# Rewriting a four-layer attention kernel: features on partitions, blocks of tokens through both layer kinds, softmax without a max pass

## The chip, the cores and the metric

One core of a Trainium2 chip. The metric is the device time of one execution in microseconds (us), slowest core; with one core that is the core. Each kernel ran several times beside runs of the kernel before on the same chip. Engines: PE is TensorE (PEld its weight loads), DVE is VectorE, ACT is ScalarE, POOL is GpSimd, SP is SyncE.

## The reference, cut to what matters

`x` is 2048 tokens by 512 features, bf16, 32 heads of 16. Four layers A, B, A, B, each with a layer norm before it and a residual after it.

```python
def _A_ref(x, wqkv, w_phi, wo):                 # linear attention
    q, k, v = ...                               # x @ wqkv, split into 32 heads of 16
    pq, pk = q @ w_phi, k @ w_phi               # per head
    phi_q = concat([softmax(pq), softmax(-pq)]) # 32 features per head
    phi_k = concat([softmax(pk), softmax(-pk)])
    kv, z = phi_k.T @ v, phi_k.sum(tokens)      # over ALL tokens
    o = (phi_q @ kv) / (phi_q @ z + 1e-6)
    return o @ wo
def _B_ref(x, wqkv, wo):                        # window of 8 tokens, every second one back
    logits[s, w] = q[s] . k[s - 2 * w] * 16 ** -0.5   # masked where s - 2w < 0
    o[s] = sum_w softmax(logits[s])[w] * v[s - 2 * w]
    return o @ wo
x = x + _A_ref(_layernorm(x), ...)   # then B, A, B
```

Layer A holds a barrier: no numerator before the key-value sum of all tokens is complete.

## The kernel before

Tokens sit on partitions: 128 tokens, 512 features along the free dimension, four such tiles to a "quad". One layer runs after the other.

```python
def s1():                                   # layer A: max and min of each head's 16, then subtract
    nc.vector.tensor_tensor(out=mm[:, 0], in0=v[:, :, 0:8, :], in1=v[:, :, 8:16, :], op=ALU.max)
    nc.vector.tensor_tensor(out=mm[:, 1], in0=v[:, :, 0:8, :], in1=v[:, :, 8:16, :], op=ALU.min)
    # ... three more tree steps for each sign, then two subtractions into dd (cut)
def s_a():                                  # layer B: logits of one tile
    nc.vector.tensor_tensor(out=prod, in0=st["Q"][:, i:i + 1, :].to_broadcast([P, NW, D]),
                            in1=Kall[:, _win(j), :], op=ALU.mult)          # 4096 wide
    for d in range(nd_):                    # sum over a head's 16 by identity matmuls, 256 columns
        nc.tensor.matmul(lg[:, i, :, :], lhsT=ident[:], rhs=prod[:, :, d * H:(d + 1) * H], ...)
def s_c():                                  # layer B: values
    nc.vector.tensor_tensor(out=pav, in0=..., in1=attn[...], op=ALU.mult)  # 4096 wide
    for cb in range(NB):
        for w in range(NW):                 # 32 identity matmuls of 128 columns
            nc.tensor.matmul(oTp[:, cb, :], lhsT=pavf[:, w, cb * P:(cb + 1) * P], rhs=ident[:], ...)
def residual_out(oT, Wo, j):
    # 4 matmuls with Wo, a fifth with the identity adds x, ScalarE copies the sum back (cut)
```

A shifted token lies on another partition, so keys and values also pass through shifted-row copies by DMA.

## Time and profile before

| | before |
|---|---|
| median of the first runs (three, and one more beside the changed kernel) | 567.5 us (565.6 to 569.8) |
| PE / DVE / ACT busy | 429.7 / 410.8 / 315.4 us |
| granted TensorE clock, profiled run | 0.91 |

### The profile page before, as it was taken

To read this page: it belongs to the slowest core of one execution; us is meant where nothing else is said; L and a number is where in the kernel's file an instruction comes from. 1 tells how busy PE (TensorE), PEld (TensorE's weight loads), DVE (VectorE), ACT (ScalarE), POOL (GpSimd) and SP (SyncE) were. 2 spreads that over 40 slices of the span, in tenths; PEclk is the share of its full clock that TensorE was granted. 3 is DMA by queue.
4 is the path that set the end of the run, shared out by engine and by line. 5 is a ranking of instruction groups with operands and counts; after the bars stand their busy time and mean duration, and the time that the engine had idled before them with its cause. 6 is when DMAs were issued, how large, how long until landed. Compare 5 with 4: busy or idle time off the path is not lost.

```text
span 567.9 us, 7855 instructions
## 1 busy us (share of the span) xinstructions
PE 429.7 (76%) x3153; PEld 265.6 (47%) x3196; DVE 410.8 (72%) x582; ACT 315.4 (56%) x529; POOL 2.7 (0%) x16
## 2 busy tenths in 40 slices
PE   0337778607897999999898687633797999999983
PEld 0213334307443666656763243223553566666762
DVE  1975799986563489886994599997672669584970
ACT  0086787832497346283458867843488535454241
POOL 1000000000000000000000000000000000000000
PEclk9999797855898999999999888966898999999998
DMA  9851030344255302022013003313544322002003
GB/s 239 203 118 34 1 74 1 74 74 111 55 135 128 75 2 65 2 62 42 1 39 70 5 2 74 74 45 74 107 105 112 80 56 59 8 14 53 1 1 149
DMA packets 98020, 37.22 MB, mean 66 GB/s; under 512 B 88512, under 2 KB 97216, under 8 KB 97728
## 3 DMA queue, kind: packets, MB, share of 16 engines
q1 hardware_dynamic: 96320, 35.66, 27.2%
q10 hardware_dynamic: 1664, 1.07, 0.8%
q8 instruction: 25, 0.41, 0.3%
q14 instruction: 11, 0.09, 0.0%
HBM read 5.26 MB, written 2.10 MB: 13 GB/s over the span
## 4 chain that ended last, share of the span: by engine, by line
DVE 39%; PE 30%; ACT 19%; issue 7%; DMA 3%; SPq 1%; ACTq 0%; DVEq 0%
PE ps_arena L298 11%; PE ps_arena L364 6%; DVE arena L355 6%; DVE arena L524 5%; PE ps_arena L306 5%; ACT arena L282 5%; DVE arena L406 5%; PE ps_arena L415 4%; ACT arena L505 3%; DVE arena L498 3%; DVE arena L496 3%; PE ps_arena L572 2%; ACT arena L300 2%; DVE stat L250 2%; ACT x_sb L310 2%
## 5 line engine op out<-in xcount | busy, mean ns | idle before, releaser
L298 PEld LDWEIGHTS <-arena 128*128 128x128 bf16 x768 | 78.6, 103 | 159.4 <-issue 74.6
L300 ACT CAST arena<-ps_arena 128x512 bf16<-128x512 f32 x192 | 110.5, 584 | 61.8 <-PE ps_arena L298 56.5
L298 PE MATMUL ps_arena<-WA,arena 128*128 128x512 bf16 x375 | 101.1, 426 | 50.1 <-ACT arena L300 37.2
L355 DVE TENSOR_TENSOR arena<-arena 128x4096 bf16<-128x4096 bf16 x32 | 71.8, 2286 | 35.3 <-ACT arena L300 33.0
L298 PE MATMUL ps_arena<-WB,arena 128*128 128x512 bf16 x372 | 90.0, 388 | 8.5 <-ACT arena L300 7.8
L406 DVE TENSOR_TENSOR arena<-arena 128x4096 bf16<-128x4096 bf16 x32 | 71.5, 2285 | 0.4
L505 ACT ACTIVATE arena<-arena 128x4096 bf16<-128x4096 bf16 x16 | 57.9, 3618 | 15.4 <-DVE arena L498 15.1
L415 PE MATMUL ps_arena<-ident,arena 128*128 128x128 bf16 x1024 | 63.1, 219 | 1.8 <-DVE arena L406 1.7
L415 PEld LDWEIGHTS <-arena 128*128 128x128 bf16 x1024 | 59.5, 98 | 10.4 <-DVE arena L406 3.8
L364 PE MATMUL ps_arena<-arena,ident 128*128 128x256 bf16 x512 | 60.5, 272 | 1.7 <-DVE arena L355 0.7
L250 DVE BATCH_NORM_STATS2 stat<-x_sb 128x6 f32<-128x512 bf16 x64 | 43.4, 684 | 24.8 <-ACT x_sb L310 24.6
L364 PEld LDWEIGHTS <-ident 128*128 128x128 bf16 x512 | 50.0, 98 | 13.7 <-issue 5.4
L310 ACT CAST x_sb<-ps_arena 128x512 bf16<-128x512 f32 x64 | 37.1, 580 | 34.5 <-PE ps_arena L309 34.5
L282 ACT ACTIVATE arena<-x_sb,nmr,rstd 128x512 bf16<-128x512 bf16 x64 | 49.3, 809 | 5.3 <-DVE nmr L274 4.8
L536 PE MATMUL ps_arena<-arena 128*128 128x136 bf16 x256 | 22.6, 265 | 30.7 <-DVE arena L524 30.6
L524 DVE TENSOR_TENSOR arena<-arena 128x4096 bf16<-128x4096 bf16 x16 | 36.6, 2286 | 5.4 <-ACT arena L522 5.4
L306 PEld LDWEIGHTS <-arena 128*128 128x128 bf16 x256 | 22.5, 99 | 33.8 <-ACT arena L419 11.6
L536 PEld LDWEIGHTS <-arena 128*128 128x128 bf16 x256 | 21.4, 121 | 34.2 <-DVE arena L524 33.1
L306 PE MATMUL ps_arena<-WoB,arena 128*128 128x512 bf16 x113 | 29.9, 381 | 8.2 <-ACT arena L419 6.0
L306 PE MATMUL ps_arena<-WoA,arena 128*128 128x512 bf16 x124 | 33.8, 387 | 0.5 <-issue 0.2
L572 PE MATMUL ps_arena<-arena 128*128 128x136 bf16 x256 | 25.5, 263 | 11.3 <-DVE arena L582 7.8
L377 ACT CAST arena<-ps_arena 128x1024 bf16<-128x1024 f32 x8 | 8.1, 1012 | 42.0 <-PE ps_arena L367 42.0
(61 smaller groups left out, 355.6 us busy)
## 6 DMA issues: line engine op xcount, KB each, us to landing
arena<-arena SPq DMA_DIRECT2D x8, 448.0 KB
arena<-arena SPq DMA_DIRECT2D x8, 336.0 KB
x_sb<-in_A_x_dram SPq DMA_DIRECT2D x1, 2048.0 KB
out_dram<-x_sb SPq DMA_DIRECT2D x1, 2048.0 KB
arena<-in_B_wqkv_dram SPq DMA_DIRECT2D x1, 1536.0 KB
arena<-arena SPq DMA_DIRECT2D x8, 105.0 KB
arena<-in_A_wqkv_dram ACTq DMA_DIRECT2D x1, 512.0 KB
arena<-arena SPq DMA_TRANSPOSE x32
```

Of the source, the lines that this page charges most:

```text
L250: nc.vector.bn_stats(out=stat[:, i, :], in_=x_sb[:, j, :])
L282: nc.scalar.activation(out=xn[:, i, :], in_=x_sb[:, j, :], func=ACT.Identity, scale=st["rstd"][:, i:i + 1], bias=st["nmr"][:, i:i + 1])
L298: nc.tensor.matmul(ps, lhsT=XNT[:, POS[j], c, :], rhs=W[:, c, col0:col0 + D], start=(c == 0), stop=(c == NB - 1))
L300: nc.scalar.copy(out=dst, in_=ps)
L306: nc.tensor.matmul(y, lhsT=oT[:, c, :], rhs=Wo[:, c, :], start=(c == 0), stop=(c == NB - 1 and not pe_res))
L310: nc.scalar.copy(out=x_sb[:, j, :], in_=y)
L355: nc.vector.tensor_tensor(out=prod, in0=st["Q"][:, i:i + 1, :].to_broadcast([P, NW, D]), in1=Kall[:, _win(j), :], op=ALU.mult)
L364: nc.tensor.matmul(lg[:, i, :, :], lhsT=ident[:], rhs=prod[:, :, d * H:(d + 1) * H], start=(d == 0), stop=(d == nd_ - 1 and not masked))
L406: nc.vector.tensor_tensor(out=pav, in0=Vall[:, _win(j), :].rearrange("p w (d h) -> p w d h", h=H), in1=attn[:, j, :, :].unsqueeze(2).to_br ...
L415: nc.tensor.matmul(oTp[:, cb, :], lhsT=pavf[:, w, cb * P:(cb + 1) * P], rhs=ident[:], start=(w == 0), stop=(w == NW - 1))
L505: nc.scalar.activation(out=ee, in_=st["dd"], func=ACT.Exp)
L524: nc.vector.tensor_tensor(out=phi, in0=ee, in1=rsb.to_broadcast([P, 2, G, DH, 8]), op=ALU.mult)
```

## The change

The intent: put features on partitions, so that a shifted token is a shifted column and needs no copy; let indicator matmuls sum over the features of a head; drop the max pass of both softmaxes (a check at the end sends unfit data to the old kernel, kept as a general path); cut the tokens into four blocks of 512 and lead each block from A into B and on into the next A, with the order of each engine's instructions set by hand through virtual times. The core of the diff, cut:

```diff
+class _Fast:
+    def g_a1(self, L, b):                       # keys and values of block b, layer A
+        for t in range(4):                      # ... projection into pk (cut)
+            nc.scalar.activation(out=E[:, t, 0, :], in_=pk[:], func=ACT.Exp)
+            nc.scalar.activation(out=E[:, t, 1, :], in_=pk[:], func=ACT.Exp, scale=-1.0)
+        # ... head sums on VectorE, scaling of E, then key-value sums over the block (cut)
+    def g_a2(self, L, b):                       # queries
+        # ... projection, two exponentials per chunk from PSUM (cut)
+        yield 0.5
+        S = self.ps()                           # head sums by 32-column indicator matmuls
+    def g_a3(self, L, b):                       # denominators, then scaling of the queries
+    def g_out(self, key, b, Wo, last, dt):
+        for t in range(4):                      # ... 4 matmuls with Wo into y (cut)
+            nc.vector.scalar_tensor_tensor(out=xb[:, t, :], in0=y[:], scalar=1.0, in1=xb[:, t, :],
+                                           op0=ALU.mult, op1=ALU.add, accum_out=sums[:, t:t + 1])
+            if t < 3:
+                yield dt
+        yield 0.8
+        for t in range(4):                      # layer norm: squares with their sum on ScalarE
+            nc.scalar.activation(out=sqd[:], in_=xb[:, t, :], func=ACT.Square, bias=nmean[:, t:t + 1],
+                                 accum_out=ss[:, t:t + 1])
+    def g_b2(self, L, b, dt):                   # logits and softmax of layer B
+        for c in range(NB + 1):                 # ... product with the shifted view of K (cut)
+            nc.tensor.matmul(lg[hf][32 * g:32 * g + 32, :], lhsT=self.indQK[:],
+                             rhs=prods[c - 1][:, hf * 4 + g, :], ..., tile_position=(0, 32 * g))
+        nc.scalar.activation(out=E[:, hf, :], in_=lg[hf][:], func=ACT.Exp, scale=..., accum_out=...)
+        yield 1.5
+        den = self.ps()                         # denominator matmul, 1 / den, PT = E / den
+        # 8 DMAs from SyncE spread PT over the partitions of each head: Pbc (cut)
+    def g_b3(self, L, b, dt):                   # values
+        nc.vector.tensor_tensor(out=pav[:], in0=Pbc[:], in1=self.win(KV, 1, c), op=ALU.mult)
+        for w in range(NW):
+            nc.tensor.matmul(po[:], lhsT=self.ident[:], rhs=pavs[c - 1][:, w, :], ...)
+    def run(self):                              # virtual start times of all blocks and stages (cut)
+        go("wbound", self.g_call(self.weight_bound), T0 + 60)   # GpSimd squares weights for the check
+        go("b4_%d%d" % (L, b), self.g_out("A%d" % (L + 1), b, self.WoB, last, 2.75), t4, ...)
+    with tc.If(redo > 0):
+        _general_path(...)                      # the kernel before
```

A `yield 1.3` lets 1.3 us of virtual time pass before the rest of that stage is issued. It moves an instruction in its engine's queue; by itself it makes nothing wait. (`rstd` below is the reciprocal standard deviation of a layer norm, and "virtual time" exists only while the program is built.)

## The prediction

> **What bounds the kernel now.** I read the page's busy rows first, then the chain that ended last, then the costliest groups, then the trace cut into stretches by layer, and last the chain in order of time, to see the real spacing of matmuls.
>
> ```profile
> PE 429.7 (76%) x3153; PEld 265.6 (47%) x3196; DVE 410.8 (72%) x582; ACT 315.4 (56%) x529; POOL 2.7 (0%) x16
> PEclk9999797855898999999999888966898999999998
> DVE 39%; PE 30%; ACT 19%; issue 7%; DMA 3%; SPq 1%; ACTq 0%; DVEq 0%
> ```
>
> No engine is above 76%, and the chain changes hands between three engines: the bound changes by stage. The stretches say which:
>
> ```profile
> 72.00:130.00 58.00, 32.70 (x192) 17.77 (x192) 54.77 (x85) 39.49 (x44) 0.41 (x2) 0.79 0.26 55
> 130.00:160.00 30.00, 24.61 (x169) 16.82 (x170) 19.35 (x39) 14.30 (x44) 0.00 (x0) 0.72 0.40 89
> 160.00:180.00 20.00, 16.38 (x79) 7.45 (x81) 8.96 (x23) 17.32 (x36) 0.00 (x0) 0.95 0.54 122
> 445.00:555.00 110.00, 104.06 (x953) 73.25 (x963) 81.33 (x63) 47.23 (x81) 0.00 (x0) 1.00 0.12 26
> ```
>
> Columns: length, then PE, PEld, DVE, ACT, POOL busy, granted clock, DMA. In layer A (72 to 130) DVE is busy 54.8 of 58 us and PE runs at clock 0.79; between layers (130 to 180) nobody is full; in layer B (445 to 555) PE is busy 104 of 110 us at clock 1.00. So: A is DVE's, B is PE's, and the seams belong to latency.
>
> ```profile
> L355 DVE TENSOR_TENSOR arena<-arena 128x4096 bf16<-128x4096 bf16 x32 | 71.8, 2286 | 35.3 <-ACT arena L300 33.0
> L505 ACT ACTIVATE arena<-arena 128x4096 bf16<-128x4096 bf16 x16 | 57.9, 3618 | 15.4 <-DVE arena L498 15.1
> L250 DVE BATCH_NORM_STATS2 stat<-x_sb 128x6 f32<-128x512 bf16 x64 | 43.4, 684 | 24.8 <-ACT x_sb L310 24.6
> L300 ACT CAST arena<-ps_arena 128x512 bf16<-128x512 f32 x192 | 110.5, 584 | 61.8 <-PE ps_arena L298 56.5
> L582 DVE TENSOR_TENSOR arena<-ps_arena,rden 128x512 bf16<-128x512 f32 x32 | 21.2, 687 | 12.9 <-ACT rden L581 12.7
> ```
>
> These give unit prices: a 4096-wide bf16 product 2.29 us (2.24 back to back, 71.8/32), 512 from PSUM on DVE 0.69, on ACT 0.58. A matmul's "mean ns" is a modelled latency, so I take PE prices from dense runs in the chain:
>
> ```profile
> 193.19 1.75 PE ps_arena L364 x16
> 262.60 2.59 PE ps_arena L298 x12
> 477.56 1.80 PE ps_arena L415 x32
> ```
>
> 1.75/16 = 109 ns for 256 columns, 2.59/12 = 216 ns for 512, 1.80/32 = 56 ns for 128.
>
> **What the Trainium skill says.** (1) "VectorE: DVE Perf Modes", the perf-mode tier table: two-tensor bf16 ops reach twice the base rate in SBUF and only the base rate with a PSUM operand; one-source ops reach four times. The trace agrees on the first two: 4096 in 2286 ns, 512 from PSUM in 687. The third I use for the new normalisation (estimate 0.29 us per 512); no row here shows it. (2) "TensorE: Matmul & The Clock Gate", back-to-back issue gap: N/2.4 + 2.5 ns warm. 109, 216 and 56 ns agree. (3) Same page, Part 3 on packing: four matmuls of 32 rows gave 3.07 times, three of 32 columns 2.38 times. The new head sums rest on this; no run here shows it. (4) Same page, Part 1: PE falls to half clock after idle windows. The 0.72 of the seam against 1.00 in B fits.
>
> **The change part by part.** It is a rewrite: features sit on partitions, tokens come in four blocks of 512, and one layer's B runs block by block into the next layer's A. Counts are from the instruction listing.
>
> PE. Matmuls of 512 columns: 768 projections, 64 numerators, 256 output projections, 256 identity sums of the value products, 24 others = 1368, by 0.216 = 295 us. Key-value products 256 of 129 columns by 0.062 = 16. Logit sums 256 of 32 by 512: 55 us if each takes the whole array, about 18 at three-fold sharing. Indicator sums and broadcasts 768 of 128 columns: 43 at 56 ns, I take 38. Fold 4. Sum **371 us** (413 without sharing). Before, by the same prices: 1088 of 512 = 235, 540 of 256 = 59, 1056 of 128 = 59, 512 of 136 = 32, sum 385. PE work hardly falls: the residual matmuls and the 512 wide logit sums leave, the value sums double in columns.
>
> DVE. Kept: 64 products, 143 us. Gone: max/min trees and subtractions of A (88 us in seven groups), the query half of the A softmax sums (40), most of the B softmax (21), three quarters of the mean/variance work (41). New: 64 query scalings from PSUM by 0.69 = 44; 64 residual adds from PSUM, 48 with the sum output; 64 normalisations by 0.29 = 19; small ones 25. Sum of durations about **343** against 433 before by the same adding up (which showed as 411 busy, as neighbours overlap).
>
> ACT. Gone: the 58 us of exponentials over both signs, 49 of normalising, 37 of residual copies. New: 128 exponentials straight from PSUM by 0.58 = 75, 48 squares by about 0.8 = 38. Sum about **282** (315 before).
>
> Transfers. The shifted-row copies leave; eight broadcasts of 128 KB per block come. Issue of the old shifted copies took a median 0.68 us each, so eight take about 5.5, plus about 2 to land: 7 to 8 us from probabilities to the first value product. In DVE's order other work fills this for three blocks, but for the last block of each B layer only one product (2.3 us) stands between: a stall of about 5 to 6, twice.
>
> Time then by stage, since barriers remain where the key-value sum of all tokens is needed.
> Stage 1, to the first barrier. Loads plus first normalisation plus transpose: about 21 us (before, the first projection came 19 us after the statistics could start, and x arrives sooner in quarters). Then four blocks, each ACT 14.2, PE 13.8, DVE 10: 57 at best, 60 with gaps, 4 of tail. **85**.
> Stage 2, A's second half, B, next A's first half. From barrier to first B projection a latency chain: sums 2.2, denominators 2.4, eight scalings 5.5, numerators and output 7, squares and rstd 4, the next block's eight scalings ahead in DVE's order 5.5, normalise and transpose 5: near 29 us with the broadcast matmuls, PE half idle. Then PE work 133 (four B projections 41.6, logits 11, value sums 27.6, output 10, rest of A 18, next A of two blocks 25) against DVE 122: PE-bound, at 95% 140. Then the last two blocks of next A: 10 us of normalise latency, some of it covered, and 28 of PE work against 27 of ACT: 33. **202**.
> Stage 3, the same without next A: 29, then PE 108 and DVE 112 balanced, at 92% 121, the broadcast stall partly inside, last projection, store and flag 8. **158**.
> Sum **445 us**, 0.78 of before.
>
> What gives the 123 us: about 15 from the start, about 75 from layer A (its DVE work falls and half of each boundary now lies beside B), the rest from the seams. B itself gives little: its PE work stays.
>
> **The rivals.** R1, no sharing of the array by the 32-wide matmuls: PE gets 42 us more, about 30 on the path in stages 2 and 3: 475. For: each carries its own weight load, and the before trace has none like it. Against: the skill's figures. R2, in-order coupling: three engines at 75 to 85% with fixed orders, so each late one stops the others; the old B window reached 95% PE, but with one dominant engine. At 85% in both windows 475 to 485. R3, the hand order is well tuned, PE reaches 97% and the A to B latency hides: 405 to 415. R4, the check at the end sends the kernel into the general path: about 1000 us. The thresholds are far from such data and counts up to 512 are exact in bf16; 1%. R5, the transfers bound it: DMA stood at 28% of 16 engines before and bytes fall; unlikely.
>
> **Range and chances.** Centre 445; R1 and R2 pull to 485, R3 to 410: range 410 to 485. Even R1 and R2 together (some 515) stay under 556, so faster 0.97, same 0.02, slower 0.01.
>
> **What would show it.** Right: PE is the busiest engine and leads the chain; DVE busy near 325, ACT near 280; first projection near 21 us; PE full at clock near 1.0 in the two B windows with clock dips only at the two barriers; 32-row logit matmuls starting under 100 ns apart; the last block's first value product waiting 5 us on a transfer. Wrong: logit matmuls 216 ns apart (R1); PE and DVE both under 80% inside B with short waits on each other (R2); a barrier-to-B time far from 29; residual adds or squares priced well off 0.75 and 0.8; general-path lines in the trace (R4).

## The result, and the profile after

The changed kernel took 517.83 us in the median (516.86 to 518.35, four runs), the kernel before 567.45 (four runs, one of them beside it): ratio 0.912, 95% interval 0.909 to 0.915. A ratio here is the mean of one kernel's fast runs over the mean of the other's of the same rounds, so not quite the ratio of medians. The gain is 50 us where 123 were predicted, and the time lies outside the range. The page of the changed kernel, busy row, clock and chain:

```profile
PE 401.8 (78%) x2713; PEld 180.2 (35%) x2713; DVE 326.1 (63%) x482; ACT 262.7 (51%) x559; POOL 22.0 (4%) x40
PEclk9888889778979899899799969868896879999987
PE 53%; DVE 26%; ACT 10%; DMA 5%; issue 3%; SPq 2%; DVEq 0%; ACTq 0%
```

DVE has 326 us (325 were predicted), ACT 263 (280). No line of the general path shows. PE leads the chain, as predicted, but it is busy only 78% of the span, and the clock dips in nearly every part of it, not at two barriers alone. The same trace cut by stage; the columns are those of the prediction (length, PE, PEld, DVE, ACT, POOL, clock, DMA):

```profile
19.80:93.30 73.50, 62.48 (x478) 33.74 (x479) 32.97 (x56) 48.77 (x102) 18.15 (x17) 0.89 0.19 44
93.30:121.80 28.50, 16.61 (x197) 7.09 (x186) 17.13 (x40) 9.87 (x22) 0.00 (x0) 0.70 0.10 19
121.80:283.60 161.80, 139.11 (x813) 57.25 (x814) 116.08 (x144) 92.84 (x199) 0.68 (x4) 0.94 0.20 43
283.60:333.10 49.50, 38.61 (x328) 20.76 (x330) 19.14 (x37) 32.78 (x72) 0.30 (x2) 0.86 0.12 22
333.10:363.50 30.40, 15.84 (x196) 6.90 (x184) 18.44 (x43) 9.59 (x22) 0.00 (x0) 0.77 0.10 19
363.50:502.60 139.10, 117.20 (x653) 46.19 (x654) 103.21 (x115) 62.72 (x134) 0.00 (x0) 0.92 0.23 50
502.60:515.60 13.00, 5.14 (x25) 2.25 (x23) 4.37 (x8) 0.58 (x1) 0.00 (x0) 0.78 0.27 87
```

The cuts are the first projection, the barrier, the first projection of B, the end of B's last value sums, the second barrier, and so on. Beside the prediction:

| stretch | predicted | measured | difference |
|---|---|---|---|
| to the first barrier | 85 | 93.3 | +8.3 |
| barrier to B, twice | 29 + 29 | 28.5 + 30.4 | +0.9 |
| first B window | 140 | 161.8 | +21.8 |
| last two blocks of the next A | 33 | 49.5 | +16.5 |
| second B window | 121 | 139.1 | +18.1 |
| end | 8 | 13.0 | +5.0 |

With the 2.2 us between the profiled span (515.6) and the median time these make the 73 us. In the first window PE is busy 139 us where I had put 133 of work, and idle 22.7 us where my "95%" left 7. In the second it is busy 117 for 108 of work, and idle 21.9 us for 13. So of the 40 us that the two windows are too long, 15 are more busy time of PE and 25 more idle time. DVE is at 72 and 74% of the two windows. So no engine is full.

The prices of the new instructions, and the sharing of the array, can be read at once. First two of the costliest groups, then two neighbours of the timeline (start, length, engine, line):

```profile
L228 DVE SCALAR_TENSOR_TENSOR x<-ps,x 128x512 bf16<-128x512 f32 x48 | 32.7, 689 | 52.6 <-PE ps L222 52.6
L242 ACT ACTIVATE sqd<-x,nmean 128x512 bf16<-128x512 bf16 x48 | 34.7, 722 | 28.5 <-DVE nmean L237 27.4
```

```profile
177.13 0.62 PE L443 MATMUL ps<-prod,maskQ 128*32 128x512 bf16 x8
177.68 0.60 PE L417 MATMUL ps<-xnT,WB 128*128 128x512 bf16 x2
```

The residual add takes 689 ns, the square 722 (each with a second record that reads the accumulator, below). Eight logit matmuls of 32 columns by 512 start at 177.13, and the next line starts 0.55 us later: 69 ns each, where one that takes the whole array has 216 (the dense price that the prediction read). The rival without sharing (R1) is out.

Where PE waits is the question. Here is PE at one of four like places (the bracket is the idle time before), then ScalarE at the same time:

```profile
169.14 1.01 PE L456 MATMUL ps<-E,indDen 128*128 128x512 bf16 x2 [4.98 <-DVE E L452]
169.95 7.25 PE L417 MATMUL ps<-xnT,WB 128*128 128x512 bf16 x28
```

```profile
163.80 0.72 ACT L242 ACTIVATE sqd<-x,nmean 128x512 bf16<-128x512 bf16 x1 [1.40 <-DVE nmean L237]
164.43 0.19 ACT L242 ACTIVATION_READ_ACCUMULATOR sqd<-x,nmean 128x1 f32 x1
...
167.63 0.58 ACT L449 ACTIVATE E<-ps 128x512 bf16<-128x512 f32 x1
```

The logits are complete at 163. ScalarE first makes four squares of another block's layer norm, with rstd 3.8 us, and only then the softmax exponentials. The denominator matmul (L456) stands at the head of PE's queue and waits 4.98 us for them (in the first block by way of VectorE's mask product, L452), while 28 projections (L417), before which the profile shows no wait, stand behind it. They then take 7.25 us where 28 x 0.216 = 6.0 was the dense price.

### The profile page after: what moved, and what is told of

Read it like the earlier page. It is cut to its first block, busy times and chain, and to the rows that moved or that the text cites. A ratio compares the mean times of both kernels' runs of the same rounds, so it can differ in the third digit from the quotient of the medians.

```text
span 515.6 us, 6841 instructions
## 1 busy us (share of the span) xinstructions
PE 401.8 (78%) x2713; PEld 180.2 (35%) x2713; DVE 326.1 (63%) x482; ACT 262.7 (51%) x559; POOL 22.0 (4%) x40
## 4 chain that ended last, share of the span: by engine, by line
PE 53%; DVE 26%; ACT 10%; DMA 5%; issue 3%; SPq 2%; DVEq 0%; ACTq 0%
PE ps L417 14%; PE ps L489 8%; PE ps L222 7%; PE ps L263 5%; DVE Eq L386 5%; DVE prod L438 5%; PE ps L271 5%; ACT sqd L242 4%; PE ps L296 4%; DVE Ek L290 4%; PE ps L311 3%; DVE x L228 3%; PE ps L397 3%; DVE pav L485 3%; DMA xnT<-xn 2%
## 5 line engine op out<-in xcount | busy, mean ns | idle before, releaser
L417 PE MATMUL ps<-xnT,WB 128*128 128x512 bf16 x384 | 101.3, 400 | 3.2 <-DMA xnT<-xn 2.7
L485 DVE TENSOR_TENSOR pav<-Pbc,KV 128x4096 bf16<-128x4096 bf16 x32 | 72.3, 2287 | 10.6 <-DMA Pbc<-PT 10.2
L489 PE MATMUL ps<-pav,ident 128*128 128x512 bf16 x256 | 64.8, 401 | 10.2 <-DVE pav L485 10.2
L438 DVE TENSOR_TENSOR prod<-QT,KV 128x4096 bf16<-128x4096 bf16 x32 | 72.7, 2286 | 0.0
L417 PEld LDWEIGHTS <-WB 128*128 128x128 bf16 x384 | 36.6, 101 | 57.3 <-issue 18.9
L419 ACT CAST KV<-ps 128x512 bf16<-128x512 f32 x64 | 37.0, 593 | 24.2 <-PE ps L417 24.2
L242 ACT ACTIVATE sqd<-x,nmean 128x512 bf16<-128x512 bf16 x48 | 34.7, 722 | 28.5 <-DVE nmean L237 27.4
L263 PE MATMUL ps<-WA,xnT 128*128 128x512 bf16 x128 | 36.9, 435 | 8.0 <-DMA xnT<-xn 8.0
L386 DVE TENSOR_TENSOR Eq<-ps,Eq 128x512 bf16<-128x512 f32 x64 | 39.4, 683 | 1.8 <-PE ps L381 1.6
L315 ACT ACTIVATE Eq<-ps 128x512 bf16<-128x512 f32 x64 | 34.6, 594 | 8.2 <-PE ps L311 8.2
L271 PE MATMUL ps<-WA,xnT 128*128 128x512 bf16 x128 | 31.7, 379 | 0.0
L222 PE MATMUL ps<-WoB,oT 128*128 128x512 bf16 x128 | 31.6, 379 | 0.0
```

Source lines behind the costliest of these rows:

```text
L222: nc.tensor.matmul(y[:], lhsT=oT[:, c, t * P:(t + 1) * P], rhs=Wo[:, c, :], start=(c == 0), stop=(c == NB - 1))
L242: nc.scalar.activation(out=sqd[:], in_=xb[:, t, :], func=ACT.Square, bias=nmean[:, t:t + 1], accum_out=ss[:, t:t + 1])
L263: nc.tensor.matmul(pk[:], lhsT=xnT[:, t, k, :], rhs=WA[:, k, D:2 * D], start=(k == 0), stop=(k == NB - 1))
L271: nc.tensor.matmul(pv[:], lhsT=xnT[:, t, k, :], rhs=WA[:, k, 2 * D:3 * D], start=(k == 0), stop=(k == NB - 1))
L386: nc.vector.tensor_tensor(out=ev, in0=pb[t][:].rearrange("p (a i) -> p a i", a=NB), in1=ev, op=ALU.mult)
L417: nc.tensor.matmul(pp[:], lhsT=WB[:, k, i, c, :], rhs=xnT[:, :, k, :], start=(k == 0), stop=(k == NB - 1))
```

## The experiments

Theories. A, mine: PE's work bounds the windows. B: the fixed orders couple PE, DVE and ACT, so each short wait stops work that is ready. C: the idle gaps drop the clock, and this costs most. Each run lasted 3 rounds (the last two 5). "Against" is the median less 517.83. The runs were on several chips; the median of the kernel before lay between 567.5 and 568.1 us in every group, so medians may be compared.

| run | median us | against | ratio to before, 95% interval |
|---|---|---|---|
| whole array for logits | 539.85 | +22.0 | 0.9505 (0.9469 to 0.9541) |
| half the value sums | 501.14 | -16.7 | 0.8820 (0.8791 to 0.8850) |
| half the value products | 508.51 | -9.3 | 0.8956 (0.8933 to 0.8980) |
| both halves | 484.84 | -33.0 | 0.8541 (0.8517 to 0.8566) |
| filler matmuls | 504.99 | -12.8 | 0.8879 (0.8850 to 0.8908) |
| before, no max pass | 542.43 | +24.6 | 0.9540 (0.9512 to 0.9568) |
| squares later | 523.76 | +5.9 | 0.9245 (0.9195 to 0.9294) |
| stage 1 order | 509.06 | -8.8 | 0.8958 (0.8943 to 0.8973) |
| earlier output projection | 515.93 | -1.9 | 0.9075 (0.9059 to 0.9090) |
| denominators later | 512.60 | -5.2 | 0.9033 (0.9008 to 0.9059) |
| stage 1 and output projection | 507.36 | -10.5 | 0.8937 (0.8902 to 0.8972) |
| four order edits | 512.87 | -5.0 | 0.9007 (0.8959 to 0.9054) |
| and squares later by one step | 517.46 | -0.4 | 0.9122 (0.9083 to 0.9160) |
| and split broadcasts | 512.25 | -5.6 | 0.9022 (0.8998 to 0.9046) |
| and filler matmuls | 510.60 | -7.2 | 0.8989 (0.8966 to 0.9012) |
| combined, GpSimd later | 505.29 | -12.5 | 0.8892 (0.8858 to 0.8925) |
| combined, no GpSimd | 500.94 | -16.9 | 0.8818 (0.8795 to 0.8842) |

### What does a microsecond of each engine cost?

The whole array for the logit sums:

```diff
-nc.tensor.matmul(lg[hf][32 * g:32 * g + 32, :], lhsT=self.indQK[:], ..., tile_position=(0, 32 * g))
+nc.tensor.matmul(lg[hf][:], lhsT=self.indW[:, g, :], ..., start=(c == 1 and g == 0), stop=(c == NB and g == 3))
```

> The logit sums take the whole array: four 128-column indicator matrices, each zero outside its 32 columns, accumulate into one bank. The result stays right. At 216 ns in place of the 69 ns seen, 256 such matmuls add 256 x 0.147 = 37.6 us of TensorE work. Theory A, TensorE's work is the bound in the two B windows: time rises by 30 to 37 us (about 550). Theory B, waits of the fixed order set the time and TensorE has slack beside them: rises by 5 to 20 us. If the gain of sharing the array was no gain at all: within 5 us.

Measured +22.0 us for 37.6 us of work: 0.59 us per us, between the two theories. Sharing the array is worth 22 us.

Half of the value sums (result wrong):

```diff
-for w in range(NW):
+for w in range(0, NW, 2):
```

> Half of the identity sums of the value products are left out (128 matmuls of 512 columns, 128 x 0.216 = 27.6 us), wrong result on purpose; VectorE still makes every product, and all transfers stay. Theory A, TensorE's work is the bound: 22 to 27 us less (about 493). Theory B, waits: 10 us less or smaller, with VectorE and ScalarE waits unchanged.

Measured -16.7 us for 27.6: 0.60 per us, the same slope from the other side. PE's work counts, but not fully, and no theory as I had stated it fits. Then VectorE (wrong):

```diff
-nc.vector.tensor_tensor(out=pav[:], in0=Pbc[:], in1=self.win(KV, 1, c), op=ALU.mult)
+nc.vector.tensor_tensor(out=pav[:, 0:4, :], in0=Pbc[:, 0:4, :], in1=self.win(KV, 1, c, 4), op=ALU.mult)
-rhs=pavs[c - 1][:, w, :]
+rhs=pavs[c - 1][:, w % 4, :]
```

> Only 4 of the 8 value products of each block and column chunk are made on VectorE (32 x 1.14 = 36.5 us of VectorE work less), and each is read twice by the identity sums, so TensorE does the same work; wrong result on purpose. Theory A, TensorE's work is the bound and VectorE has slack: 5 us less or smaller. Theory B, the windows are coupled, each engine in turn on the path: 12 to 22 us less, like the 16.7 us that taking 27.6 us from TensorE gave.

Measured -9.3 us: 0.26 per us. Its five times spread from 506.6 to 514.2, more than others; the likely reason turns up below. It lies in stage 1, so this slope is rough: the fastest of the five gives 0.31. Then both halves together:

```diff
+nc.vector.tensor_tensor(out=pav[:, 0:4, :], ...)        # 4 of 8 products, as in the last run
+for w in range(4):                                      # and 4 of 8 identity sums
```

> Half of the value products and half of the identity sums are left out together (36.5 us of VectorE and 27.6 us of TensorE work); wrong result on purpose. If a single engine bounds the windows, both together bring no more than the better one alone. Theory B, coupling: about the sum of the two alone or more, 30 to 45 us less than the changed kernel (about 480).

Measured -33.0 us, more than the 26.0 of the two alone. The two B windows, first of the half value sums, then of the half products, then of both:

```profile
122.00:275.50 153.50, 128.21 (x749) 51.40 (x750) 115.42 (x143) 91.63 (x197) 0.68 (x4) 0.91 0.21 45
353.60:486.60 133.00, 107.82 (x589) 40.62 (x590) 103.11 (x115) 62.43 (x133) 0.00 (x0) 0.86 0.23 52
```

```profile
126.70:286.00 159.30, 138.91 (x813) 57.46 (x814) 99.47 (x144) 92.80 (x199) 0.68 (x4) 0.94 0.20 44
365.60:499.30 133.70, 116.65 (x653) 46.12 (x654) 86.39 (x115) 62.69 (x133) 0.00 (x0) 0.91 0.23 52
```

```profile
121.40:267.80 146.40, 125.12 (x749) 50.80 (x750) 98.68 (x143) 91.54 (x197) 0.68 (x4) 0.93 0.22 47
346.10:469.60 123.50, 103.85 (x589) 40.17 (x590) 86.30 (x115) 62.27 (x133) 0.00 (x0) 0.89 0.24 56
```

Against 161.8 and 139.1 us, the first saves 8.3 and 6.1, the second 2.5 and 5.4, the third 15.4 and 15.6: 31.0 us in the windows, where the two alone saved 14.4 and 7.9. The windows lie outside stage 1, so the spread of the second run doesn't touch this. Neither engine alone bounds a window; each takes over where the other is relieved. PE's idle time stays near 20 us in the third as well (146.4 - 125.1 and 123.5 - 103.9). That is what coupling means here: shorter work, same waits. Whether the fixed orders couple the engines, or the data that one needs from the other, these runs don't tell.

### The cold clock

Filler matmuls into a bank nobody reads, put into PE's order where it idled (seven places, 206 matmuls):

```diff
+def fill(self, n):
+    f = self.ps()
+    for i in range(n):
+        self.nc.tensor.matmul(f[:], lhsT=self.ident[:], rhs=self.WoA[:, i % NB, :], ...)
+self.fill(12)      # for example ahead of the denominator matmul of the first block
```

> Filler matmuls (512 columns, into a bank nobody reads) are put in TensorE's order at the places where it stood idle: before the transposed first block, before the key-value and head sums, before the denominators. The result stays right. Theory C, the cold clock after idle gaps costs most of the missing time: granted clock rises from 0.89 to about 0.97 and the time falls by 25 to 40 us. If the waits themselves cost it and the cold clock little: the clock rises, the time stays within 8 us either way, or is longer where a filler lies on the path.

The clock rose from 0.892 to 0.954 and the time fell by 12.8 us: real, but half of the least that theory C asked. Cut at the same events as above, the stretches that gained are stage 1 (3.3 us), the two ways from barrier to B (2.5 and 2.1), the tail of stage 2 (3.1) and the second window (2.1); the first window lost 1.4, probably where fillers stood ahead of work that had become ready.

### How much is the missing max pass?

The kernel before with its max and min trees and subtractions deleted:

```diff
-nc.vector.tensor_tensor(out=mm[:, 0], ..., op=ALU.max)      # and the rest of the trees, both layers
-nc.scalar.activation(out=ee, in_=st["dd"], func=ACT.Exp)
+nc.scalar.activation(out=ee[:, 0], in_=v, func=ACT.Exp)
+nc.scalar.activation(out=ee[:, 1], in_=v, func=ACT.Exp, scale=-1.0)
```

> The kernel before with one part of the change alone: both softmaxes without their max and min passes, exponentials of the values as they are; everything else as before. The result stays right on this data. About 88 us of VectorE work leaves layer A and about 14 leaves layer B. My estimate: layer A's VectorE-bound stretch loses most of it, layer B stays with TensorE: about 525 us. If it reaches 518 or less, the layout change brought nothing beyond it; if it stays above 550, the max passes were hidden.

Measured 542.43 us: 25 less than before, about half of the 50 us of the whole change, though DVE lost 87 us of busy time (411 to 324). That is its worth in the old kernel; what it is worth inside the new one was not tried. My estimate of 525 missed for the same reason as the prediction: I let the DVE-bound stretch shrink to what DVE needed, but in this run's profile ACT stood at 76% from 60 to 120 us (45.8 of 60), PE at 63% and DVE at 58%: none was full.

### Waits mended one by one

Squares after the softmax exponentials, for three kinds of block:

```diff
-yield 0.8
+yield hold         # 6.0 for the last block of A and the first two of B, else 0.8
```

> Only the emission order moves: the four squares, logarithm and rstd of the layer norm of other blocks are issued on ScalarE after the softmax exponentials instead of ahead of them, so the denominator matmul at the head of TensorE's queue is not held up by them. Theory B, head-of-line waits: the four waits of about 5 us for exponentials shrink to under 1.5 us and 12 to 20 us leave the time (about 500). Theory A, TensorE's work: within 5 us. A miss is possible where the later squares hold up the next block's first projection.

A miss, and an instructive one. From the list of PE's waits (waiting line, what it waited for, total us, times, longest), three lines of the changed kernel and three of this one:

```profile
PE ps L456 <- DVE E L452: 10.0, 2, 5.0
PE ps L456 <- ACT E L449: 9.7, 5, 5.0
PE ps L263 <- DMA xnT<-xn: 8.0, 1, 8.0
```

```profile
PE ps L263 <- DMA xnT<-xn: 24.1, 3, 8.4
PE ps L443 <- DVE prod L438: 12.8, 9, 4.0
PE ps L456 <- ACT E L449: 1.6, 4, 0.6
```

The denominator waits went, 17 us of them, as expected. In their place the next projections waited for the transposed block (8.0 to 24.1 us), because the later squares made the layer norm later, and the logit sums for products (4.8 to 12.8). All of PE's listed waits together were 105 us in the changed kernel and 112 here: they moved and did not go. A step of 2.5 in place of 6.0, on top of four other edits that come below, did no better:

```diff
+yield hold         # 2.5 for the same three kinds of block
```

> The four order edits, and the squares of three blocks moved behind the softmax exponentials by one step only (not six as in the miss). Theory B: the remaining denominator waits of 3.4 and 5.0 us go and no transfer wait replaces them: 4 to 8 us less than the four edits alone. If the squares' follow-up, the transposed block, is again what the next projections wait for: within 2 us or slower.

Measured 517.46 against 512.87 without it: slower by 4.6. So in the other versions the squares stay ahead of the exponentials. The matmul that waits for both can be moved instead:

```diff
+if b < 3:
+    yield 4.5
 yield 1.5
 den = self.ps()
```

> The denominator matmul of the first three blocks of each B layer, and the first block's mask product, are issued later in the fixed order, behind independent projections and value sums; the squares stay where they are. Theory B, head-of-line waits: the four waits of 3.8 to 5.0 us disappear without the new transfer waits that moving the squares brought; 8 to 16 us less (about 506). If TensorE's waits only move elsewhere: within 4 us.

Measured -5.2, less than expected. Of the four long waits the edit removed that of the third block (3.76 us); in the first block of each B layer 4.98 us fell only to 3.39; and the fourth, of 4.98 us, belongs to the last block of the first B, which the edit (`b < 3`) leaves out. That wait is still there in the best version below. Stage 1 next. Its PE in the changed kernel:

```profile
53.67 0.73 PE L322 MATMUL ps<-Eq,indS 128*32 128x128 bf16 x20 [1.27 <-ACT Eq L315]
55.80 1.77 PE L296 MATMUL ps<-vaug,Ek 128*128 128x129 bf16 x16 [1.41 <-DVE Ek L290]
57.37 1.91 PE L263 MATMUL ps<-WA,xnT 128*128 128x512 bf16 x4
59.07 1.09 PE L296 MATMUL ps<-vaug,Ek 128*128 128x129 bf16 x13
```

Head sums and key-value sums each wait over 1 us for ScalarE and VectorE; then from 57.37 to 59.07 four projections take 1.70 us, 425 ns each, twice their price. No single wait was longer than 1.5 us, but from 52.00 to 55.80 PE was busy for only 1.04 us of 3.80, and then the profile has its granted clock at 0.57 (55.80 to 57.37) and 0.50 (57.37 to 59.07); "cold" below means such a lowered clock. Issuing both behind the first projections of the next block:

```diff
-yield 0.5
+yield 3.5 if L == 0 and b < 3 else 0.5        # ahead of the head sums
-yield 2.5
+yield 5.5 if L == 0 and b < 3 else 2.5        # ahead of the key-value sums
```

> Only the emission order of stage 1 moves: key-value sums and head sums of a block are issued on TensorE after the first projections of the next block, so the exponentials they wait for are there. Theory B: the period of a block falls from 17.5 to about 15 us, 8 to 12 us in all (about 508). If ScalarE's own work sets the period of stage 1: within 3 us.

Measured -8.8, as theory B said. The stretch of stage 1 in this kernel:

```profile
19.80:85.10 65.30, 58.12 (x470) 31.74 (x475) 36.08 (x56) 48.82 (x102) 18.14 (x17) 0.93 0.21 49
```

65.3 us in place of 73.5, with PE busy 58 instead of 62: nearly the same matmuls, warmer (clock 0.93 in place of 0.89). Then the third block's output projection, issued at once:

```diff
-self.g_out("A%d" % (L + 1), b, self.WoB, last, 2.75)
+self.g_out("A%d" % (L + 1), b, self.WoB, last, 0.9 if b == 2 else 2.75)
```

> The output projection of the third block of each B layer is issued ahead of the value sums of the fourth block instead of spread among later work, so it fills the wait of TensorE for the broadcast transfers of the last block (5 us), and the third block's layer norm starts earlier. Theory B: 8 to 18 us less (about 505), most of it at the end of stage 2, where the wait of 8.0 us for the transposed block shrinks. If the later work was filled by it anyway: within 4 us.

Measured -1.9: a miss. In its profile the tail of stage 2 did shrink by 4.9 us (49.5 to 44.6), but the windows gave about 4 back. (That profile is of the slowest of the four runs, with a loss of 4.5 us in stage 1 which is explained below and isn't the edit's.) Both edits together, stage 1 and output projection:

> The two order edits of stage 1 and of the third block's output projection together. If they are independent: 8.8 + 1.9 = about 11 us less than the changed kernel (about 507).

Measured -10.5, the sum of the two (10.7). The broadcasts of the last block, half of them issued from ScalarE, on top of four edits:

```diff
-nc.sync.dma_start(out=Pbc[:, hf * 4 + g, :], in_=src)
+q = nc.scalar if b == 3 and g % 2 else nc.sync
+q.dma_start(out=Pbc[:, hf * 4 + g, :], in_=src)
```

> The four order edits, and the eight broadcast transfers of the last block of each B layer issued half from SyncE and half from ScalarE. Eight issues on one queue took 5.1 us; four take 2.6. Expect the wait before the last block's value product to fall from about 5 to about 2.5 us, twice: 3 to 5 us less than the four edits alone. If the landing of the transfers and not their issue sets it: within 1 us.

Measured 512.25 against 512.87: no gain. PE's longest wait for a value product fell only from 5.5 to 4.8 us. In the second B the eight issues did end sooner, 3.4 us after the first began in place of 5.1; but those from ScalarE landed 3.8 us after issue in the median, against 2.7 from SyncE, and that took back most of it.

### Why four edits were slower than two

```diff
-go("wbound", self.g_call(self.weight_bound), T0 + 60)
+go("wbound", self.g_call(self.weight_bound), T0 + 30)      # and the three edits above
```

> Four order edits together: stage 1's sums later, the third block's output projection earlier, the denominators of three blocks later, and GpSimd's squares of the weights half way through stage 1 earlier, where VectorE has no product of two inputs to make (in two profiles such a product took 5.7 us beside them in place of 2.3). If the waits add: 10.5 + 5.2 + about 1 = 16 to 18 us less than the changed kernel (about 500) and the spread of the runs under 2 us. If each mended wait is replaced by another: no better than 505.

512.87, worse than the 507.36 of two edits, and stage 1 back at 72 us. The timeline of this kernel, and then of the one with two edits:

```profile
23.53 7.16 POOL L171 TENSOR_TENSOR sq<-WA 128x2048 bf16<-128x2048 bf16 x2 [20.00 <-ACT WA L552]
23.88 3.27 DVE L209 COPY mean<-mv 128x4 f32<-128x4 f32 x1
27.26 4.64 DVE L184 TENSOR_SCALAR xn<-x,mean,rstd 128x512 bf16<-128x512 bf16 x4
```

```profile
23.59 0.17 DVE L209 COPY mean<-mv 128x4 f32<-128x4 f32 x1
25.27 1.38 DVE L184 TENSOR_SCALAR xn<-x,mean,rstd 128x512 bf16<-128x512 bf16 x4 [1.51 <-ACT rstd L196]
```

A copy of four numbers takes 3.27 us in place of 0.17, and four normalisations 4.64 in place of 1.38, while GpSimd multiplies the weights. The Trainium skill, "SBUF — State Buffer", § Who interferes with whom, states it: VectorE and GpSimd share a pair of memory ports under an exclusive lock, held for the whole instruction, and where both need it the second to ask "fully blocks". The trace agrees: the copy ends at 27.15, about when the first of GpSimd's two products (7.16 us for both) is over. By chance the same meeting takes place in other kernels. In the profile of the earlier output projection:

```profile
53.68 5.74 DVE L290 TENSOR_TENSOR Ek<-Ek,rk 128x4096 bf16<-128x4096 bf16 x1 [2.72 <-ACT rk L288]
```

The key scaling, 2.29 us elsewhere, takes 5.74, beside GpSimd's squares that start at the same 53.68. The profile of the half value products has it too (its eight key scalings average 2.71 us); it is the likely cause of the wide spread of those two. I had moved the work into a worse place. Next, with that work after the first barrier:

```diff
+go("wbound", self.g_call(self.weight_bound), T0 + 104)
+0.9 if b == 2 and L == 0 else 2.75     # earlier output projection in the first B only
+self.fill(...)                         # behind the barriers and before the last block's value sums only
                                        # stage 1 and denominator edits as before
```

> Stage 1's sums later, denominators later, the third block's output projection earlier in the first B layer only, filler matmuls only behind the two barriers and before the last block's value sums, and GpSimd's squares of the weights after the first barrier. If the collision of GpSimd with VectorE's two-input sums was what stage 1 lost in the four edits: stage 1 back at 65 us (73 there), and with 2 us at each barrier and 2 in the second window: 495 to 500 us, less than any version so far. If the collision was not it: stage 1 stays at 70 us or more and the time at 504 to 508.

505.29, short of what I expected, and within the 504 to 508 that I had set for "the collision was not it"; stage 1 took 68.5 us, between the two marks. The trace says why: GpSimd started as soon as its buffers came free, at 74.8 us, before the barrier, and met the last key scaling (4.68 us; PE waited 3.5 us for it). Emission order had not held it, because GpSimd had nothing to wait for. The last run gives the squares to ScalarE, behind the barrier:

```diff
-nc.gpsimd.tensor_tensor(out=sq[:], in0=w, in1=w, op=ALU.mult)
+nc.scalar.activation(out=sq[:], in_=w, func=ACT.Square)
```

> As the last run, with the squares of the weights on ScalarE behind the first barrier (two of about 1.8 us in its idle time there) and not on GpSimd. If the meeting of GpSimd and VectorE was the loss: stage 1 at 64 to 66 us, no VectorE product of 4096 above 2.4 us, the times within 2 us of each other, and 500 to 503 us. If not: stage 1 at 68 us or more, 504 to 507.

500.94 us (499.89 to 501.86), stage 1 at 65.6 us, as expected; this is the best version that still computes the right result, 3% under the changed kernel and 12% under the one before. (Eight fillers went where the weight matmuls now stand.) Its profiled run has the clock at 0.937 (0.892 in the changed kernel). Between this run and the last, the GpSimd work is nearly the only difference (the eight fillers and the place of the weight matmuls are the rest), and of the 3.6 us between the two profiles 3.2 lie in stage 1. So the collision cost some 3 to 4 us there. The two B windows of this best version:

```profile
112.50:276.60 164.10, 145.97 (x820) 59.89 (x831) 116.21 (x145) 91.67 (x198) 0.67 (x4) 0.92 0.20 42
349.80:487.20 137.40, 116.26 (x656) 46.46 (x665) 103.28 (x115) 62.00 (x133) 0.00 (x0) 0.95 0.23 50
```

Together 301.5 us, where the changed kernel has 300.9. The 17 us came from stage 1, the ways from barrier to B and the tail of stage 2; the windows are as long as before.

One more run put fillers on top of the four edits (the places of the filler run, without stage 1 of the first A):

```diff
+self.fill(12)      # and so on, as in the filler run; in the sums only where L == 1 and b > 1
```

> The four order edits, and the filler matmuls at the places still idle (before the denominators, the numerators of the first two blocks, the transposed third block, the last block's value sums), none in stage 1. Theory C says the cold clock costs as much after the order edits as before outside stage 1: granted clock 0.95 or more, 7 to 10 us less than the four edits alone. If the waits that caused it are gone: within 3 us.

510.60 against 512.87, clock 0.944 against 0.897: these fillers brought about 2 us where I expected 7 to 10. What the cold clock itself still costs can't be read from this, since a filler can also stand ahead of ready work.

## Why the prediction was wrong

**What held.** The busy sums: DVE 326 for 325, ACT 263 for 280, PE work 133 and 108 in the windows for 139 and 117 busy, part of it at a cold clock. The prices: 0.69 plus 0.08 us for the residual add (0.75), 0.72 plus 0.19 for the square (0.8; they start 0.85 apart). The way from barrier to B: 28.5 and 30.4 for 29. The stall of the last block on its broadcasts: the two waits of VectorE make 10.2 us in all for "5 to 6, twice" (the transfers landed 2.7 us after issue in the median, for "about 2"). The first projection at 19.8 us for 21. The sharing of the array (69 ns). Neither R1, R4 nor R5 came.

Some of this agreement hides slips in the working. The parts named for the way from barrier to B add to 31.6 us, not 29; in the trace the squares (from 111.37 to 115.29) run beside the next block's scalings (from 111.25), so the 29 was partly luck. The parts named for DVE take 433 to 379, not 343: the list leaves out the old division (L582, 21 us) and the query half of another product (L524, half of 37 us). The durations of the changed kernel do add to 343. The normalisation, estimated at 0.29 us, took 0.41 (four in a row 1.38). R4 says that counts up to 512 are exact in bf16: 512 is, but an odd count such as 511 is not, and no run tried whether the check catches one bad column alone.

**What failed.** First, the terms "PE-bound, at 95% 140" and "at 92% 121". I took the work of the busiest engine (PE's 133 us, then DVE's 112) and divided by an efficiency near that of the old B window, which reached 95% with one dominant engine. I had named this rival (R2: "three engines at 75 to 85% with fixed orders, so each late one stops the others") and priced it at 475 to 485; the windows came out with PE at 86 and 84%, DVE at 72 and 74% (so R2's own sign, both under 80%, was not met to the letter). The half-work runs show that PE does not bound the windows alone: PE's work gives 0.6 us per us, DVE's 0.26, both together more than their sum. Together the windows are 40 of the 73 us. What I put for R2 was too little, and did not follow from its own terms either: 133 and 108 us at 85% make 156 and 127, which lifts the 445 to 468. It was charged to the windows alone, with PE's work at warm prices.

Second, "60 with gaps, 4 of tail" of stage 1: from the first projection to the barrier it took 73.5 and not 64. The term rests on ACT's 14.2 us a block, 57 in all; but ACT was busy for only 48.8 us of it, and PE for 62.5. The order run showed 8.2 us of the stage to be head and key-value sums at the head of PE's queue. GpSimd beside VectorE costs a further 4 us or so where the two meet, which the prediction had not thought of; in the changed kernel's own profile they hardly did (its key scalings average 2.33 us).

Third, "the last two blocks of next A ... 33": it took 49.5. Of the 16.5 us too much, 10.6 are busy time of PE (38.6 for 28) and 5.9 idle time. Work was left out: the tail also held 24 matmuls of the output projection (5.2 us at the dense price) and the key-value and head sums of three blocks, not two (96 of each). What remains of the busy time, some 3 us, was run at a granted clock of 0.86; the idle time holds one wait of 8.0 us for a transposed block. The earlier output projection saved 4.9 us in the tail, and the windows gave about 4 back.

Fourth, every PE price was a warm price. The skill's clock rule stood among the points of the prediction, but its cost was set to zero; "clock near 1.0" in the windows came out as 0.94 and 0.92. The fillers show about 13 us of it in the changed kernel; this overlaps with the three terms above, which hold cold time too.

**What stays open.** The order edits, the fillers and the squares moved off GpSimd recover 17 of the 73 us, none of it in the two windows. 18 and 21 us of PE's idle time remain there in the best version. No order edit made a window more than 3.6 us shorter (the denominators, in the first one). So that the fixed order is what couples the engines is shown for stage 1 and not for the windows: whether another order frees them, or only less dependence between the engines, the runs don't tell; nor were the 5 us at the end examined. The best version was not run without its fillers.

## What to carry to other kernels

When a change takes the dominant engine away, don't reuse the efficiency that the dominant engine allowed: with three engines at 60 to 80% in fixed orders, price the waits at the head of each queue. Here each us of work taken from one engine brought 0.6 us (PE) or about 0.3 (DVE). Read what stands behind a waiting instruction in its own queue; if it is ready, move the waiting one, and look for the wait that appears next. And treat an idle engine as occupied if it shares a port: GpSimd's "free" work held up one VectorE product by 3.5 us.

## What the Trainium skill lacked or had wrong

- "TensorE: Matmul & The Clock Gate", Part 1, gives idle gaps of more than about 3.4 us as what makes TensorE cold, and frequent micro-idles as a second mode, without the length of such gaps. Here two waits of 1.27 and 1.41 us within 4 us, with PE busy 1.04 of 3.80 us around them, were followed by projections at 425 ns instead of 216.
- Same page, Part 3: its column packing has three tiles (2.38 times). Four groups of 32 columns, each matmul with its own weight load, ran at 69 ns per 512 columns against 216, 3.1 times; the page has no row for it.
- "VectorE: DVE Perf Modes" says that an operation with accumulator output is two instructions, and "ScalarE: Activation LUTs" that there is an accumulator output; I found no cost on either. The second record took 0.08 us on VectorE and 0.19 us on ScalarE, where four in a row lay ahead of the softmax.
